# Input units in 64-row halves beside the scores: an attention and bilinear feed-forward kernel on one Trainium2 core

## The chip, the cores and the metric

The kernel runs on one core of a Trainium2 chip. The time is the device time in microseconds (us) of one execution, and lower is better. Before the change, the median of six executions is 417.81 us (415.93 to 419.45).

Engines are named as the profile names them: PE is TensorE (matmuls, transposes), PEld its loading of weights, DVE is VectorE, ACT is ScalarE, POOL is GpSimd, SP is SyncE. POOL and SP here mostly issue DMA transfers. PE writes only to PSUM, which has eight banks, each of 128 partitions by 512 fp32 values.

## The reference

```
B, H, S, D = 8, 8, 576, 64                      # q, k, v: [B, H, S, D]
scores = (q @ k^T) / sqrt(D) + bias[bucket(|i-j|)]   # one bias table a head
attn   = exp(scores - max) / sum
x      = (attn @ v) laid out as [B*S, H*D] = [4608, 512]
out    = ((x @ w_a) * (x @ w_b)) @ w_out         # d_model 512, d_ff 1536
```

## The kernel before, in words

**Pairs and slots.** Two heads of a batch entry make a pair; there are 32 pairs (`NP`), four to a batch entry. The loop over `s` from 4 to 32 is what this text calls slots: slot `s` computes the scores of pair `s` and the weighted values (`av`) of pair `s - 1`. The sequence of 576 is cut into four blocks of 128 and a tail of 64.

**Scores of a pair.** `qk1(p, t)` (line 334) multiplies key block `t` with all 512 queries, for the two heads at once: head 0 lies on partitions 0 to 63 and head 1 on 64 to 127, so there are two matmuls of 64 rows, one for each half of PE's rows, into two banks (line 342). `qk(p, t0)` does two blocks. `ex` (line 353) takes the exponential on ACT into a bf16 tile `at` of a pool of 8. `mul` (line 361) multiplies a band of it by exp(bias) on DVE. The `sc` pool has two buffers of two banks each.

**Tail.** `qk_tail` (lines 364 to 375) takes the main keys against the tail queries (line 367: four matmuls of 128 rows and 128 columns, both heads in one matmul, the operand padded with zeros), the tail keys against the main queries (line 370: one of 512 columns), and tail against tail (line 373: two of 64 columns into a bank `qktt`). `ex_tail` takes the exponentials of `qktt` and of the rest, `mul_tail` applies the bias. For pairs below 12 `qktt` lies in the bank TR, from 12 (`R3`) on in AV.

**Values and norm.** `av(p, jq)` (lines 403 and 412) multiplies the exponentials with v and a column of ones, for query blocks 0 to 2 into one bank and 3 to 4 into another. `norm` divides by the sums on DVE (a reciprocal on line 448, a product on line 449) into `XG`. `t_x` transposes `XG` into the feed-forward input `xn`: on PE with copies (`c_x`) for the first pairs, with DMA transposes on SP's queue for pairs 8 to 30 (`XD`). `t_q`, `c_q`, `t_k` and `c_k` make the transposed q and k of the next pair in PE for the first three batch entries (up to slot 10); later ones come from DMA transposes (`turn`).

**Feed-forward units.** There are nine chunks of 512 tokens (eight batch entries without their tails, and one of all tails). A chunk has 24 input units (`ff_a` and `ff_b` for each of 12 blocks of d_ff) and 12 output units (`ff_o`, four token blocks in three parts). Each unit is four matmuls of 128 rows and 512 columns. An a unit ends with ACT's copy `ha` out of PSUM (line 518), a b unit with the product `g = pb * ha` on DVE (line 523), and the third part of an output block with ACT's copy `ob` (line 546) and a store on SP's queue. There is one set of 12 tiles `g`, and the units run in one fixed order, chunk by chunk.

**Order.** Nothing schedules: the order in which instructions are written out is the order on each engine. The list `steps` of each slot mixes the attention steps with places `U`, and a quota of units (9 a slot from slot 9 on) is spread over these places. In slots 5 to 31 the scores come in two runs: `qk(s, 0)`, some units and av blocks, `qk(s, 2)`, more units and steps, then the tail. What is left of the units after the last slot runs by itself at the end.

**Banks.** Eight PSUM banks: four for `sc`, one AV, one TR, two FF. Units use the two FF banks in turn, and from slot 12 on (`ring3`) also TR for every third.

Of the kernel before, what the change touches and what calls it, by code (L numbers as in the profile page):

```python
# [13 lines left out]
def kernel(  # L14
# [11 lines left out]
    nc = tc.nc  # L26
# [22 lines left out]
    obp = ctx.enter_context(tc.tile_pool(name="obp", bufs=4))  # L49
    atp = ctx.enter_context(tc.tile_pool(name="atp", bufs=8))  # L50
    ps_sc = ctx.enter_context(tc.tile_pool(name="ps_sc", bufs=2, space=bass.MemoryType.PSUM))
# [57 lines left out]
    NW = 3  # L109
    R3 = 12  # L110
    WC = DF // NW
# [3 lines left out]
    xn_sb = [wpool.tile([128, 3 * SM + ST * B], BF16, name=f"xn{mc}") for mc in range(NMC)]  # L115
    g_sb = [wpool.tile([128, DM], BF16, name=f"g{df}") for df in range(NDF)]

# [149 lines left out]
    def kTt_(p):  # L267
        b, hp = divmod(p, 4)
        return KT[p % 2][:, SM:SM + 128] if early(b) else KTt[b % 2][:, hp, :]
# [9 lines left out]
    def bank(where, dt, name):  # L279
        return where[0].tile([128, 512 if dt is FP32 else 1024], dt, tag=where[1], name=name)  # L280
# [83 lines left out]
    def qk_tail(p):  # L364
        ps = ps_sc.tile([128, 2, 512], FP32, tag="sc", name=f"qkt{p}")
        for t in range(NM):
            nc.tensor.matmul(  # L367
                out=ps[:, 0, :].rearrange("p (h t c) -> p h t c", h=2, t=NM)[:, :, t, :],
                lhsT=kT_(p, t), rhs=qTt_(p), start=True, stop=True)
        nc.tensor.matmul(out=ps[:, 1, :], lhsT=kTt_(p), rhs=qT_(p), start=True, stop=True)  # L370
        pt = bank(TR if p < R3 else AV, FP32, f"qktt{p}")
        for hh in range(2):
            nc.tensor.matmul(out=pt[:, 0:ST], lhsT=kTt_(p), rhs=qTt_(p)[:, ST * hh:ST * hh + ST],  # L373
                             start=(hh == 0), stop=(hh == 1))
        st[p]["ps"] = (ps, pt)

    def ex_tail(p):
        ps, pt = st[p]["ps"]
        at = att_sb[p % 2]
        nc.scalar.activation(out=at[:, 1024:1024 + ST], in_=pt[:, 0:ST], func=ACTF.Exp, scale=scale)  # L380
        nc.scalar.activation(out=at[:, 0:1024].rearrange("p (a x) -> p a x", a=2),  # L381
                             in_=ps[:, :, :], func=ACTF.Exp, scale=scale)

# [109 lines left out]
    ring3 = False  # L493
    turn3 = 0

    def ff_bank(name):
        nonlocal turn3
        where = FF
        if ring3:
            turn3 += 1  # L500
            where = TR if turn3 % 3 == 0 else FF
        return where[0].tile([128, 512], FP32, tag=where[1], name=name)

    MC = (0, 1, 2, 3)

    def ff_mm(c, df, w, key, m0, m1):
        if m0 == 0:
            ff[key] = ff_bank(f"{key}{c}_{df}")
        for i in range(m0, m1):
            mc = MC[i]  # L510
            nc.tensor.matmul(out=ff[key][:, :], lhsT=w[df // FW][:, mc, 128 * (df % FW):128 * (df % FW) + 128],  # L511
                             rhs=xn_sb[mc][:, xin(c)],
                             start=(i == 0), stop=(i == NMC - 1))

    def ff_a(c, df, m0=0):
        ff_mm(c, df, wa_sb, "pa", m0, NMC)
        ha = wrk.tile([128, 512], FP32, tag="ha", name=f"ha{c}_{df}")
        nc.scalar.activation(out=ha[:, :], in_=ff["pa"][:, :], func=ACTF.Copy)  # L518
        ff["ha"] = ha

    def ff_b(c, df, m0=0):
        ff_mm(c, df, wb_sb, "pb", m0, NMC)
        nc.vector.tensor_tensor(out=g_sb[df][:, :], in0=ff["pb"][:, :], in1=ff["ha"][:, :], op=MULT)  # L523

    def ff_last(c, tt):
        ob = obp.tile([128, DM], FP32, tag="ob", name=f"ob{c}_{tt}")
        for x, cols in enumerate((slice(0, 256), slice(256, 512))):
            po = ff_bank(f"po{c}_{tt}_{x}")
            for df in range(NDF):
                nc.tensor.matmul(out=po[:, cols], lhsT=g_sb[df][:, 128 * tt:128 * tt + 128],  # L530
                                 rhs=wo_sb[:, df, cols], start=(df == 0), stop=(df == NDF - 1))
            copy(None if x else nc.scalar, ob[:, cols], po[:, cols])
            for hh, eng in enumerate((nc.sync, nc.scalar)):
                r0 = S * (2 * tt + hh) + SM
                eng.dma_start(out=out[r0:r0 + ST, cols], in_=ob[64 * hh:64 * hh + 64, cols])

    def ff_o(c, tt, part):
        if part == 0:
            ff["po"] = ff_bank(f"po{c}_{tt}")
        po = ff["po"]  # L540
        for df in range(4 * part, 4 * part + 4):
            nc.tensor.matmul(out=po[:, :], lhsT=g_sb[df][:, 128 * tt:128 * tt + 128],  # L542
                             rhs=wo_sb[:, df, :], start=(df == 0), stop=(df == NDF - 1))
        if part == 2:
            ob = obp.tile([128, DM], FP32, tag="ob", name=f"ob{c}_{tt}")
            nc.scalar.activation(out=ob[:, :], in_=po[:, :], func=ACTF.Copy)  # L546
            if c < B:
                r0 = S * c + 128 * tt
                nc.sync.dma_start(out=out[r0:r0 + 128, :], in_=ob[:, :])
            else:  # L550
                for hh in range(2):
                    r0 = S * (2 * tt + hh) + SM
                    nc.sync.dma_start(out=out[r0:r0 + ST, :], in_=ob[64 * hh:64 * hh + 64, :])

    units = []
    def last(part):
        if part == 0:
            ff_last(NCH - 1, 3)

    for c in range(NCH):  # L560
        for df in range(NDF):
            m0 = 3 if c == 0 and df == 0 else 0
            units.append(lambda c=c, df=df, m0=m0: ff_a(c, df, m0))
            units.append(lambda c=c, df=df, m0=m0: ff_b(c, df, m0))
        for tt in range(4):
            for part in range(3):
                if c == NCH - 1 and tt == 3:
                    units.append(lambda part=part: last(part))
                else:
                    units.append(lambda c=c, tt=tt, part=part: ff_o(c, tt, part))  # L570
    nxt = 0

    def put_units(n):
        nonlocal nxt
        for _ in range(n):
            units[nxt]()
            nxt += 1

    ACT = nc.scalar
# [134 lines left out]
    norm(3, 3)  # L714
    ff_mm(0, 0, wa_sb, "pa", 0, 3)
    t_x(3, AV, range(3))
    t_x(3, AV, range(3, 5))
    ff_mm(0, 0, wb_sb, "pb", 0, 3)
    c_x(3)
# [16 lines left out]

    quotas = {4: 12, 5: 7, 6: 6, 7: 4, 8: 4}
    for s in range(4, NP + 1):
        new = s < NP
        U = "unit"  # L740
        A = lambda *jq: (lambda: [av(s - 1, j, AV if j < 3 or s >= R3 else TR) for j in jq])
        N = lambda j: (lambda: norm(s - 1, j))
        steps = []
        if s == R3:
            ring3 = True
        if s == 4:
# [4 lines left out]
                      lambda: mul_tail(4), U, lambda: t_q(5, TR), lambda: c_q(5), U,  # L751
                      lambda: t_k(5, AV), lambda: c_k(5), U, U]
        elif new:
            e = early((s + 1) // 4)
            steps += [lambda: qk(s, 0), lambda: ex(s, 0), U, lambda: ex(s, 1), A(0, 1, 2), N(0), U,
                      lambda: mul(s, 0)]
            av34 = [A(3, 4), N(3)]
            if s - 1 in XD:
                av34 += [lambda: t_x(s - 1), lambda: turns(s)]
            if s < R3:  # L760
                steps += av34
            steps += [U, lambda: mul(s, 1)]
            if s >= R3:
                steps += av34
            steps += [lambda: qk(s, 2), lambda: ex(s, 2), U]
            if e:
                steps += [lambda: t_q(s + 1, TR), lambda: c_q(s + 1)]
            steps += [lambda: ex(s, 3), U, lambda: mul(s, 2)]
            if e:
                steps += [lambda: t_k(s + 1, AV), lambda: c_k(s + 1)]  # L770
            steps += [U, lambda: mul(s, 3), lambda: qk_tail(s), lambda: ex_tail(s), U]
            if s - 1 not in XD:
                steps += [lambda: t_x(s - 1, TR), lambda: c_x(s - 1), lambda: turns(s)]
            steps += [U, lambda: mul_tail(s), U]
        else:
            steps += [A(0, 1, 2), N(0), U, A(3, 4), N(3), U, lambda: t_x(s - 1, AV),
                      lambda: c_x(s - 1), U, U, U, U, U, U, U]
        quota = quotas.get(s, 9)
        seen, put = 0, 0
        nu = sum(1 for x in steps if x is U)  # L780
# [47 lines left out]
```

## Time and profile before

| | |
|---|---|
| median of six executions | 417.81 us |
| the profiled execution | 415.93 us, of which the span from the first to the last instruction is 414.2 us |
| mean granted TensorE clock | 0.999 of full speed |
| busy PE / PEld / DVE / ACT / POOL | 403.2 / 207.9 / 197.2 / 245.1 / 119.4 us |
| start of slot 9 (its first score matmul) | 79.8 us |
| start of slots 10, 11, 12, 13 | 91.5, 103.3, 114.5, 125.6 us |
| start of slot 31 | 324.7 us |

The groups that matter, by line (mean length of one instruction, not the distance between two):

| line, engine | what | count | mean ns |
|---|---|---|---|
| 342 PE | scores, 64 rows by 512 columns | 256 | 382 |
| 511, 542 PE | units, 128 rows by 512 columns | 1231 | 380 |
| 367 PE | tail scores, 128 rows by 128 columns | 128 | 220 |
| 412 PE | values, 128 rows by 65 columns | 1248 | 193 |
| 353 ACT | exp of scores, 128 by 1024 | 128 | 1023 |
| 518 ACT | copy `ha`, 128 by 512 | 108 | 598 |
| 380 ACT | exp of `qktt`, 128 by 64 | 32 | 224 |
| 523 DVE | product `g`, 128 by 512 | 108 | 692 |
| 361 DVE | bias product, 128 by 512 / 128 by 768 | 64 / 64 | 418 / 551 |

The length of a matmul in the profile includes its way through the array, and the next one starts before it ends. How fast PE gets on is therefore read from the distances of starts. A few per cent of matmul records are missing from the trace, which looks like a gap of one matmul.

### The profile page before, as it was taken

What the parts mean: (1) busy time and instruction counts of PE and PEld (TensorE: products, weight loads), DVE (VectorE), ACT (ScalarE), POOL (GpSimd) and SP (SyncE); (2) the same over time, 40 slices, a digit from 0 to 9 for tenths busy, and PEclk for the clock granted to TensorE, in tenths of its full rate; (3) what the DMA queues carried; (4) which work ended last, traced back from release to release, by engine and by line L of the source; (5) the groups of instructions that cost most, each with busy time, mean ns of one, the idle gap of its engine ahead of it and who ended that gap; (6) DMA issues with size and microseconds to landing.
All of it is one profiled execution on the core that took longest, in us unless ns stands there. A gap on an engine that the chain in (4) does not pass through costs nothing.

```text
span 414.2 us, 8425 instructions
## 1 busy us (share of the span) xinstructions
PE 403.2 (97%) x3350; PEld 207.9 (50%) x3407; DVE 197.2 (48%) x485; ACT 245.1 (59%) x345; POOL 119.4 (29%) x161
## 2 busy tenths in 40 slices
PE   8899999999999999999999999999999999999996
PEld 3573555645555545555455445555555554444443
DVE  3785676556533555255524563455435540430430
ACT  4987576766766666566667665776567632322321
POOL 9989729905447001820082003000000000000000
PEclk9999999999999999999999999999999999999999
DMA  9999999999959911999099909811120002002004
GB/s 160 195 174 164 161 174 153 171 161 95 132 63 183 166 35 36 140 168 119 16 130 199 110 16 86 179 35 39 41 90 15 3 17 101 2 0 102 2 0 101
DMA packets 164935, 40.75 MB, mean 98 GB/s; under 512 B 155320, under 2 KB 160224, under 8 KB 164896
## 3 DMA queue, kind: packets, MB, share of 16 engines
q0 software_dynamic: 110448, 18.75, 64.9%
q1 hardware_dynamic: 53168, 21.03, 27.4%
q10 hardware_dynamic: 1280, 0.43, 0.5%
q8 instruction: 26, 0.43, 0.4%
q14 instruction: 13, 0.11, 0.1%
HBM read 38.77 MB, written 9.45 MB: 116 GB/s over the span
## 4 chain that ended last, share of the span: by engine, by line
PE 94%; DMA 2%; issue 1%; ACT 1%; DVE 1%; SPq 0%; ACTq 0%
PE pa L511 23%; PE pb L511 22%; PE po L542 22%; PE av L412 9%; PE qk L342 8%; PE av L403 2%; PE qkt L367 2%; PE qkt L370 1%; DMA kt<-in_k_dram 1%; DMA k<-in_k_dram 1%; ACT at L353 1%; PE trx L475 1%; PE po L530 1%; PE qktt L373 1%; PE trq L291 0%
## 5 line engine op out<-in xcount | busy, mean ns | idle before, releaser
L353 ACT ACTIVATE at<-qk 128x1024 bf16<-128x1024 f32 x128 | 126.2, 1023 | 24.0 <-PE qk L342 24.0
L523 DVE TENSOR_TENSOR g<-pb,ha 128x512 bf16<-128x512 f32 x108 | 74.7, 692 | 116.9 <-PE pb L511 101.5
L511 PE MATMUL pa<-xn,wa 128*128 128x512 bf16 x417 | 110.2, 380 | 1.1 <-issue 0.3
L511 PE MATMUL pb<-xn,wb 128*128 128x512 bf16 x411 | 109.2, 380 | 1.1 <-issue 0.2
L518 ACT ACTIVATE ha<-pa 128x512 f32<-128x512 f32 x108 | 64.6, 598 | 66.4 <-PE pa L511 65.8
L542 PE MATMUL po<-wo,g 128*128 128x512 bf16 x403 | 96.3, 380 | 1.1 <-issue 0.3
L511 PEld LDWEIGHTS <-wa 128*128 128x128 bf16 x432 | 39.1, 98 | 49.6 <-issue 9.2
L511 PEld LDWEIGHTS <-wb 128*128 128x128 bf16 x432 | 39.2, 98 | 47.8 <-issue 7.1
L361 DVE TENSOR_TENSOR at<-at,W 128x512 bf16<-128x512 bf16 (+1 forms) x128 | 59.1, 484 | 7.1 <-ACT at L353 5.5
L542 PEld LDWEIGHTS <-g 128*128 128x128 bf16 x420 | 37.8, 98 | 46.4 <-issue 7.4
L546 ACT ACTIVATE ob<-po 128x512 f32<-128x512 f32 x35 | 20.9, 597 | 60.7 <-PE po L542 58.8
L123 POOL DMA_DIRECT2D vm<-in_v_dram x32 | 28.2, 925 | 98.4 <-PE av L412 61.3
L412 PE MATMUL av<-vm,at 128*128 128x65 bf16 x992 | 43.3, 193 | 0.0
L412 PEld LDWEIGHTS <-at 128*128 128x128 bf16 x992 | 39.4, 97 | 6.2
L448 DVE RECIPROCAL rc<-av 128x6 f32<-128x6 f32 x64 | 12.0, 188 | 54.5 <-PE av L412 52.9
L403 PE MATMUL av<-vt,att 128*128 128x130 bf16 x156 | 34.7, 223 | 0.0
L381 ACT ACTIVATE att<-qkt 128x1024 bf16<-128x1024 f32 x32 | 32.6, 1020 | 0.0
L449 DVE TENSOR_TENSOR XG<-av,rc 128x384 bf16<-128x384 f32 x64 | 31.4, 491 | 2.4 <-DVE rc L448 0.2
L123 POOL DMA_DIRECT2D qn<-in_q_dram x28 | 24.4, 923 | 23.7 <-PE trq L291 16.2
L123 POOL DMA_DIRECT2D kn<-in_k_dram x28 | 24.5, 919 | 4.8 <-DMA vt<-in_v_dram 2.4
L342 PE MATMUL qk<-QTb,KTb 64*128 64x512 bf16 x160 | 24.2, 382 | 0.0
L403 PEld LDWEIGHTS <-att 128*128 128x128 bf16 x156 | 15.3, 98 | 7.4 <-issue 0.7
(121 smaller groups left out, 242.0 us busy)
## 6 DMA issues: line engine op xcount, KB each, us to landing
out_dram<-ob SPq DMA_DIRECT2D x32, 256.0 KB, 4.1
vm<-in_v_dram POOLq DMA_DIRECT2D x28, 128.0 KB, 5.8
qn<-in_q_dram POOLq DMA_DIRECT2D x24, 128.0 KB, 9.1
kn<-in_k_dram POOLq DMA_DIRECT2D x24, 128.0 KB, 9.4
wa<-in_moe_w_a_dram POOLq DMA_DIRECT2D x3, 512.0 KB, 7.0
wb<-in_moe_w_b_dram POOLq DMA_DIRECT2D x3, 512.0 KB, 9.7
wo<-in_moe_w_out_dram POOLq DMA_DIRECT2D x1, 1536.0 KB, 13.3
W<-bias_tab POOLq DMA_DIRECT2D x4, 192.0 KB, 5.1
```

The source lines that it names most:

```text
L123: nc.gpsimd.dma_start(out=(vm[b % 2][:, h0:h1, t, 0:Dh] if dst is None else dst[b % 2][:, :].rearrange("p (t h d) -> p t h d", h=H, t=NM)[ ...
L342: nc.tensor.matmul(out=ps[:, hh, :], lhsT=kT_(p, t)[r, :], rhs=qT[r, :, :], start=True, stop=True)
L353: nc.scalar.activation(out=at[:, :, :], in_=ps[:, :, :], func=ACTF.Exp, scale=scale)
L361: nc.vector.tensor_tensor(out=at[:, :, lo:hi], in0=at[:, :, lo:hi], in1=w[:, :, y:(None if z < 0 else z):-1], op=MULT)
L381: nc.scalar.activation(out=at[:, 0:1024].rearrange("p (a x) -> p a x", a=2), in_=ps[:, :, :], func=ACTF.Exp, scale=scale)
L403: nc.tensor.matmul(out=pav[:, slot, :, :], lhsT=x, rhs=vt[b // 2 % 2][:, 4 * i + hp, :, 0:Dh + 1], start=fresh, stop=True, skip_group_chec ...
L412: nc.tensor.matmul(out=pav[:, slot, hh, :], lhsT=x, rhs=vm[i][:, 2 * hp + hh, t, 0:Dh + 1], start=False, stop=True, skip_group_check=True)
L449: nc.vector.tensor_tensor(out=xg[:, j0:j0 + n, :, :], in0=pav[:, 0:n, :, 0:Dh], in1=rc.unsqueeze(3).to_broadcast([128, n, 2, Dh]), op=MULT)
L511: nc.tensor.matmul(out=ff[key][:, :], lhsT=w[df // FW][:, mc, 128 * (df % FW):128 * (df % FW) + 128], rhs=xn_sb[mc][:, xin(c)], start=(i = ...
L518: nc.scalar.activation(out=ha[:, :], in_=ff["pa"][:, :], func=ACTF.Copy)
L523: nc.vector.tensor_tensor(out=g_sb[df][:, :], in0=ff["pb"][:, :], in1=ff["ha"][:, :], op=MULT)
L542: nc.tensor.matmul(out=po[:, :], lhsT=g_sb[df][:, 128 * tt:128 * tt + 128], rhs=wo_sb[:, df, :], start=(df == 0), stop=(df == NDF - 1))
```

## The change

**What it does.** From slot 9 (`R4`) on, a slot begins with `run`: the four score blocks of the pair and the matmuls of four input units, all with 64 rows. Each unit matmul of 128 rows is split into its lower and its upper 64 rows, which add up in the same bank. Two units go together, one in an FF bank, the other in AV (first two) or TR (last two): `begin` writes the lower halves of the one beside the upper halves of the other, `end` the two remaining sets. Between them the copy `hop` on DVE reads one value of a bank of `begin`, and the matmuls of `end` wait for it. Then come the tail scores, the main keys by 64-row halves, two matmuls a key block of 64 columns, in the same run; line 370's matmul becomes two of 256 columns; and `qktt` lies in AV. The bank layout of the tail scores changes, and `ex_tail` writes them to the same places.

After it come the rest of the units as whole matmuls, the values of the pair before, and for slots 9 and 10 the transposes of the next pair. `plan` gives for each slot how many input and output units it has: 6 and 3, but (4, 3), (6, 0), (5, 0), (5, 0), (4, 3) in slots 9 to 13 and (6, 0) in slot 17. That is 189 units in slots 9 to 31, against 207 before; the other 18 run at the end. Input units are now ahead of output units by up to a chunk and a half, so there are two sets of `g`, the second one in the tiles `q32` and `k32`, which are used only in the first slots. `atp` has 10 buffers, not 8. The use of TR by every third unit (`ring3`) starts in slot 32. In slot 8 the transposes of pair 7 (`t_x`, `c_x`) come earlier in the slot.

```diff
+    def wide(p):
+        return p >= R4
...
     def qk_tail(p):
         ps = ps_sc.tile([128, 2, 512], FP32, tag="sc", name=f"qkt{p}")
-        for t in range(NM):
+        if wide(p):
+            for t in range(NM):
+                for hh in range(2):
+                    r = slice(64 * hh, 64 * hh + 64)
+                    nc.tensor.matmul(out=ps[:, hh, ST * t:ST * t + ST], lhsT=kT_(p, t)[r, :],
+                                     rhs=qTt_(p)[r, ST * hh:ST * hh + ST], start=True, stop=True)
+            for x in range(2):
+                nc.tensor.matmul(out=ps[:, x, 256:512], lhsT=kTt_(p), rhs=qT_(p)[:, 2 * x:2 * x + 2, :],
+                                 start=True, stop=True)
+        for t in range(NM if not wide(p) else 0):
...
-        pt = bank(TR if p < R3 else AV, FP32, f"qktt{p}")
+        pt = bank(AV if wide(p) else TR, FP32, f"qktt{p}")
...
+    def put_in(us, where):
+        nonlocal here
+        for u in us:
+            here = where
+            for x in u_mms(u):
+                mm(x)
+            here = None
+            u_end(u)
+
+    def begin(x, y):
+        nonlocal here
+        got = []
+        for u, where in (x, y):
+            here = where
+            got.append(u_mms(u))
+        here = None
+        for p, q_ in zip(*got):
+            mm(p, lo)
+            mm(q_, hi)
+        nc.vector.tensor_copy(out=hop[:, :], in_=got[1][0][0][0:1, 0:1])
+        return got
+
+    def end(x, y, got):
+        for p, q_ in zip(*got):
+            mm(q_, lo, False, True, True)
+            mm(p, hi, False, True, True)
+        for u in sorted((x[0], y[0]), key=lambda u: (u[2], u[0])):
+            u_end(u)
+
+    def run(s, us):
+        u, v_ = [sorted(x, reverse=True) for x in (us[0:2], us[2:4])]
+        u, v_ = list(zip(u, (FF, AV))), list(zip(v_, (FF, TR)))
+        qk1(s, 0)
+        ex(s, 0)
+        got0 = begin(*u)
+        qk1(s, 1)
+        ex(s, 1)
+        got1 = begin(*v_)
+        qk1(s, 2)
+        ex(s, 2)
+        end(*u, got0)
+        qk1(s, 3)
+        ex(s, 3)
+        end(*v_, got1)
...
+    plan = {9: (4, 3), 10: (6, 0), 11: (5, 0), 12: (5, 0), 13: (4, 3), 17: (6, 0)}
...
+        A = lambda *jq: (lambda: [av(s - 1, j, AV if j < 3 or s == NP else TR) for j in jq])
...
+        elif new and s >= R4:
+            e = early((s + 1) // 4)
+            n_in, n_out = plan.get(s, (6, 3))
+            four, rest, o = take(ins, 4), take(ins, n_in - 4), take(outs, n_out)
+            X = lambda us: [lambda: put_in(us, FF)]
+            TQ = [lambda: t_q(s + 1, TR), lambda: c_q(s + 1)] if e else []
+            TK = [lambda: t_k(s + 1, TR), lambda: c_k(s + 1)] if e else []
+            first = o[0:1] or rest[0:1]
+            rest = rest if o else rest[1:]
+            steps += [lambda: run(s, four), lambda: qk_tail(s), lambda: put_in(first, FF), lambda: ex_tail(s),
+                      lambda: mul(s, 0)] + TQ + X(o[1:2]) + [lambda: mul(s, 1)]
+            steps += TK + X(o[2:]) if o else []
+            steps += [A(0, 1, 2), N(0)]
+            steps += [] if o else TK
+            steps += X(rest[0:1]) + [lambda: mul(s, 2), A(3, 4), N(3), lambda: t_x(s - 1), lambda: turns(s)]
+            steps += X(rest[1:2]) + [lambda: mul(s, 3), lambda: mul_tail(s)]
```

`u_mms` lists a unit's matmuls, `u_end` writes its copy, product or store, `lo` and `hi` are partitions 0 to 63 and 64 to 127, `put_in` is a unit of whole matmuls, `X` one such place, `A` an av block, `N` a norm.

## The prediction

> **What bounds the kernel now.** I read the page first: the engines' busy time and the chain that ended last.
>
> ```profile
> span 414.2 us, 8425 instructions
> ...
> PE 403.2 (97%) x3350; PEld 207.9 (50%) x3407; DVE 197.2 (48%) x485; ACT 245.1 (59%) x345; POOL 119.4 (29%) x161
> ...
> PEclk9999999999999999999999999999999999999999
> ...
> PE 94%; DMA 2%; issue 1%; ACT 1%; DVE 1%; SPq 0%; ACTq 0%
> ```
>
> TensorE (PE) is 94% of the chain at full granted clock, and the other engines are little over half busy. So time comes off only where TensorE issues less or loses less between its matmuls, and every new TensorE wait is paid in full. Busy time cannot show the losses, since a record lasts 0.38 us where matmuls follow every 0.2155 us. So next I read starts of matmuls, in the timeline of one slot (a slot is one pair of heads, here slot 20): of PE, then of ACT and DVE in the same slot. Columns: start and length in us, engine, line, operation, count.
>
> ```profile
> 213.74 0.38 PE L542 MATMUL po<-wo,g 128*128 128x512 bf16 x1
> 214.05 0.39 PE L342 MATMUL qk<-QTb,KTb 64*128 64x512 bf16 x2
> ...
> 218.45 0.40 PE L412 MATMUL av<-vm,att 128*128 128x65 bf16 x8
> 218.79 0.60 PE L342 MATMUL qk<-QTb,KTb 64*128 64x512 bf16 x4
> 219.33 1.04 PE L511 MATMUL pa<-xn,wa 128*128 128x512 bf16 x4
> 220.20 1.02 PE L511 MATMUL pb<-xn,wb 128*128 128x512 bf16 x4
> 221.06 1.03 PE L511 MATMUL pa<-xn,wa 128*128 128x512 bf16 x4
> 221.93 0.39 PE L367 MATMUL qkt<-QTt,KTb 128*128 128x128 bf16 x4
> 222.15 0.38 PE L370 MATMUL qkt<-QTb,KTt 128*128 128x512 bf16 x1
> ```
>
> ```profile
> 220.40 0.60 ACT L518 ACTIVATE ha<-pa 128x512 f32<-128x512 f32 x1 [0.16 <-PE pa L511]
> 220.90 1.02 ACT L353 ACTIVATE at<-qk 128x1024 bf16<-128x1024 f32 x1
> ...
> 222.63 0.22 ACT L380 ACTIVATE att<-qktt 128x64 bf16<-128x64 f32 x1
> ```
>
> ```profile
> 221.34 0.69 DVE L523 TENSOR_TENSOR g<-pb,ha 128x512 bf16<-128x512 f32 x1 [1.80 <-PE pb L511]
> ```
>
> Four matmuls of a unit take 0.86 us (220.20 to 221.06), so one takes 0.2155. Around the 64-row scores there is a loss. From the last 128-row matmul at 213.74 to the first 64-row one at 214.05 are 0.31 us: 0.095 too many. The four 64-row matmuls of 218.79 run as two pairs, each two matmuls in the time of one (0.431 for both), yet the next unit starts 0.54 later: 0.11 too many. The unit after it starts 0.87 later, not 0.86: 0.01. One 64-row run costs 0.21 us over its work, and each slot has two. Between them TensorE does not wait: slots 13 to 31 are 11.06 us apart ((324.7 - 125.6)/18, starts of line 342). Only slots 9, 10 and 11 each show one gap of 0.15 us:
>
> ```profile
> 89.77 0.81 PE L511 MATMUL pa<-xn,wa 128*128 128x512 bf16 x3
> 90.56 1.02 PE L511 MATMUL pb<-xn,wb 128*128 128x512 bf16 x4
> ```
>
> (last start 89.77 + 0.81 - 0.38 = 90.20, next 0.36 later, 0.15 over the step).
>
> **The change, part by part, for its 23 slots (9 to 31).**
>
> *One 64-row run in place of two.* Saves 23 x 0.21 = 4.8 us. The tail halves continue this run, so the way back to 128 rows is still paid once.
>
> *Tail scores in halves.* The four matmuls of line 367 take 0.22 us (221.93 to 222.15). After it, four pairs of 64 columns. No row shows such a pair. If the two run together as in line 342, a pair takes 0.029 (the step of the 65-column matmuls of line 412: eight in 0.24 us) plus the 3 to 4 ns between the starts of a 342 pair, 0.033; if they do not, 0.058. I take the first, the nearest row in form: saving 0.22 - 0.13 = 0.09 a slot, 2.0 us; bounds 2.4 and -0.3. The Trainium skill (TensorEngine Tiling (Array Packing), Instruction Overhead) speaks against it: about 60 cycles of overhead for each matmul, so tiling should not be bought from a dimension that is already small. By the 65-column row the step at 65 columns is 0.029 us; an estimate by the page, eight matmuls of 64 columns that do not gain from pairing, would make this term nearly zero. One matmul of 512 columns as two of 256 adds nothing (the 24 of line 530 step by 0.109).
>
> *Sixteen unit matmuls as 16 pairs of halves.* Same columns streamed, if pairs follow every 0.2155 us. From the first matmul of the last pair in a run to the next 128-row one are 0.312 us, against 0.311 the other way, so a pair costs some 1 ns more than one matmul: 16 x 23 x 0.001 = 0.4 us lost. Bounds: zero, and the distance of the two pairs of a run, 0.227 us; but the first two 128-row matmuls after a run also are 0.226 apart, so I read that as a cost of starting. If it held for each pair: 4.2 us. That pairs accumulate into two banks at once is shown nowhere here.
>
> *The added copy `hop` and its waits.* The second halves wait for a VectorE copy that waits for the first halves. Four pairs and two scores lie between (6 x 0.2155 = 1.3 us); VectorE's last work of a slot (line 361, 387, 390: 0.33 + 0.16 + 0.14 between starts, behind a g of 0.61) ends some 1.8 us into the next, the wait is at 2.4. Zero; without this cover some 0.2 us each. Behind a late hop would queue the g products, and behind them the banks.
>
> *The first 128-row unit of a slot waits for a bank.* It takes the FF bank of the first b unit. Counting from the first score: pair n starts at 0.227 + 0.2155(n - 1). Third score (pair 10) 2.17; plus 0.42 to its exp (start to ACT as at 218.79 and 219.22) 2.59; the a unit's copy follows 0.90 later (the least distance of two ACT starts after an exp in the trace) at 3.49, ends 4.09; g starts 0.03 later, takes 0.69; TensorE resumes 0.06 after: 4.87. TensorE gets there at 0.227 + 19 x 0.2155 + 0.13 + 0.095 + 0.23 + 0.06 = 4.84. Wait 0.03 x 23 = 0.8 us; zero if the tail halves are slow, 1.3 if they are at their best.
>
> *The tail bank moves to AV, and a copy gets ahead of it.* In slots 10, 11 and 17, which have no output units, the first 128-row unit is an a unit, and its copy stands ahead of the tail's exp in ScalarE's in-order queue. The next av matmuls want the AV bank that this exp frees. From the unit's last start: 0.38 to its end, 0.04, 0.49 for the copy's step, 0.22 for exp (222.63), 0.05 to TensorE: 1.18, of which 0.2155 is its own step. TensorE stands 0.97 us in slots 11 and 17, and 0.75 in slot 10, where four transposes (0.22) come between: 2.7 us. Nothing hides it; the units that would have are moved to the end.
>
> *AV and TR now also hold a units.* In a full slot norm's products are done over 0.5 us before. Slots 9 to 13 have only 5 to 7 units: VectorE lags. Worked through in the same way, slot 13's first a unit waits 0.7 us for norm of slot 12 (three g of 0.61 and two multiplies of 0.33 and 0.46 stand ahead); slot 10 waits 0.3 for the K copy in TR; five others 0.13 or less: 1.6 us. In slot 9 the exps start late behind the tail of slot 8: 0.3. Together 1.9, bounds 0.5 and 3.
>
> *Hidden or neutral.* Eighteen units move from the slots to the end, where units also step by 0.86: zero. The second set of g removes a wait that TensorE does not have. POOL's v loads and the transposes on SP (3.5 us to landing) leave later in the slot, behind av, at most 6 us, with a slot or more to spare; the output stores on SP keep their count. The 0.15 gaps of slots 9 to 11 go: 0.45 us gained.
>
> **Sum.** 4.8 + 2.0 + 0.45 - 0.4 - 0.8 - 2.7 - 1.9 = 1.5 us. Span 414.2 to 412.7; the profiled execution took 415.93, so 414.4. That one was the fastest of six; on their median of 417.81: **416.3 us**.
>
> **Rivals.**
> *The waits of the short slots vanish* (ScalarE gets through earlier, or TensorE fills in): then 4.8 + 2.0 + 0.45 - 0.4 - 0.8 = 6.1, that is 411.7 us. For it: ScalarE is 59% busy. Against: its queue is in order, and the copy needs a unit that TensorE has only just finished. Chance 0.18.
> *Halves pace slower* (the other side): pairs in the run follow every 0.227 us as the measured two do, because the second load of weights or accumulation into two banks is not hidden. Price 4.2 in place of 0.4, and with the tail pairs unpaired 2.3 less a returned 0.8: the sum falls to -3.8, 421.6 us; without the tail part 420.1. It decides from 5 ns a pair, where the gain of 1.5 is gone. Against it: the weights of the second pair are loaded 11 ns after the first pair starts. The skill (TensorE: Matmul & The Clock Gate, Measured speedup vs the span model) has some 4 ns per tile and 3.07 times for four row tiles, not 4. The trace has 1 ns a pair; by the page's 4 ns, an estimate, this term would be 1.5 us and the gain nearly zero. Chance 0.25.
> *The halves do not run side by side at all*: 16 x 23 x 0.2155 = 79 us, 495 us. Pairs of line 342 start 3 to 4 ns apart, against it. Chance 0.02.
>
> **How the numbers follow.** The forecast has 0.55. A difference of 0.5% (2.1 us) is about what a measurement of this kernel can tell from none. The forecast's own range by its bounds is a gain of 3.5 to a loss of 1, with three tenths of it above 2.1. Faster: 0.18 + 0.17 = 0.35. Within: most of the rest of the forecast, 0.35, and the milder part of the slow rival, 0.05: 0.40. Slower: 0.25. Range 412.8 to 420.0: up to near the first rival, down into the second.
>
> **What would show it.** One 64-row stretch a slot with 20 pairs 0.2155 us apart; full slots some 10.8 us long for nine units; gaps near 1 us ahead of line 423 in slots 11 and 17, ended by the tail's exp; one of 0.7 in slot 13 ended by VectorE. Pairs of 0.22 us or more, or full slots over 11 us, would make it wrong on the slow side; no gaps in slots 10 to 17 on the fast side.

## The result, and the profile after

The changed kernel takes 415.22 us (median of 21 executions, 414.09 to 416.26), the kernel before 417.40 (median of 47). The ratio is 0.9948, with a 95% interval of 0.9938 to 0.9959: 2.2 us less. The forecast was 1.5 us less than a median of 417.81, 416.3 us, in a range of 412.8 to 420.0.

These lines of the changed kernel's page stand for the ones shown of before. Of them the chain looks different; the busy shares hardly moved.

```profile
span 414.2 us, 9454 instructions
...
PE 399.7 (97%) x3831; PEld 219.3 (53%) x3890; DVE 201.2 (49%) x531; ACT 243.9 (59%) x345; POOL 119.3 (29%) x161
...
PE 79%; DMA 11%; POOL 6%; issue 2%; DVE 1%; ACT 1%; POOLq 0%; DVEq 0%
```

Its span is that of before, 414.2 us, though the medians differ by 2.2. The two profiled executions stand at different ends of their kernels' scatter: before's was the fastest of 47 (415.93), the changed kernel's (415.97) among its slower ones. The DMA and POOL shares of the chain point to a load that came late ahead of slot 9. By the starts of the slots, slot 9 begins 2.67 us later: 0.79 of it lie ahead of slot 4, 1.26 in slot 7, where the transposes of K wait for the load of kn, and 0.62 in slot 8; the experiments come back to the last two. So the stretches are compared by the start of the first score matmul of each slot.

| | before | after |
|---|---|---|
| start of slot 9 | 79.75 | 82.42 |
| slot 9 to the end | 334.41 | 331.77 |
| slot 8 | 7.58 | 8.20 |
| slots 9 to 13 (before 45 units, after 30, the other 15 at the end) | 56.87 | 45.22 |
| a full slot (mean of 19 to 25) | 11.062 | 10.794 |
| slot 17 (9 units, after 6) | 11.06 | 9.16 |

The timeline of the changed kernel's slot 20 shows the run (columns as above; the places where two halves go together are two lines with one start):

```profile
190.93 0.39 PE L347 MATMUL qk<-QTb,KTb 64*128 64x512 bf16 x2
191.16 0.38 PE L538 MATMUL pb<-xn,wb 64*128 64x512 bf16 x1
191.16 0.38 PE L538 MATMUL pa<-xn,wa 64*128 64x512 bf16 x1
191.38 0.38 PE L538 MATMUL pb<-xn,wb 64*128 64x512 bf16 x1
191.38 0.38 PE L538 MATMUL pa<-xn,wa 64*128 64x512 bf16 x1
...
195.26 0.28 PE L375 MATMUL qkt<-QTt,KTb 64*128 64x64 bf16 x8
195.47 0.39 PE L378 MATMUL qkt<-QTb,KTt 128*128 128x256 bf16 x2
195.70 0.22 PE L388 MATMUL qktt<-QTt,KTt 128*128 128x64 bf16 x2
195.81 1.02 PE L538 MATMUL po<-wo,g 128*128 128x512 bf16 x3
```

Pairs start 0.216 us apart: in the 16 slots from 15 on whose halves all start together (all but slot 18), the first distance of a run is 0.226 us, and the other 304 are 215 to 217 ns, 215.8 in the mean, as are the distances of whole matmuls before. So a pair of halves costs what one whole matmul costs. The four pairs of tail halves step by 0.028 to 0.029 us, the pace of single matmuls of 65 columns before. There is one way in and one way out of the 64 rows a slot. `po` starts 0.05 us later than it could.

In slot 13 the first halves do not start together:

```profile
118.10 0.38 PE L538 MATMUL pb<-xn,wb 64*128 64x512 bf16 x1
118.80 0.39 PE L538 MATMUL pa<-xn,wa 64*128 64x512 bf16 x1 [0.32 <-DVE XG L469]
```

The half of the a unit was due beside the b half at 118.10. It came 0.70 us later, when the norm product on DVE had read its bank, AV. Over the step of 0.2155, the distance between the two starts is 0.48 us too long.

### The profile page after: what moved, and what is told of

Same layout as the page of the kernel before. It is cut to its first block, busy times and chain, and to the rows that moved or that the text cites. A ratio compares the mean times of both kernels' runs of the same rounds, so it can differ in the third digit from the quotient of the medians.

```text
span 414.2 us, 9454 instructions
## 1 busy us (share of the span) xinstructions
PE 399.7 (97%) x3831; PEld 219.3 (53%) x3890; DVE 201.2 (49%) x531; ACT 243.9 (59%) x345; POOL 119.3 (29%) x161
## 4 chain that ended last, share of the span: by engine, by line
PE 79%; DMA 11%; POOL 6%; issue 2%; DVE 1%; ACT 1%; POOLq 0%; DVEq 0%
PE po L538 21%; PE pa L538 20%; PE pb L538 20%; PE av L432 7%; PE qk L347 5%; DMA wb<-in_moe_w_b_dram 5%; DMA qn<-in_q_dram 3%; DMA vm<-in_v_dram 2%; PE av L423 2%; PE qkt L378 2%; DMA kn<-in_k_dram 1%; PE qkt L375 1%; PE po L555 1%; POOL vt L150 1%; POOL ktl L150 1%
## 5 line engine op out<-in xcount | busy, mean ns | idle before, releaser
L538 PE MATMUL pb<-xn,wb 64*128 64x512 bf16 (+1 forms) x592 | 156.7, 378 | 1.3
L538 PE MATMUL pa<-xn,wa 128*128 128x512 bf16 (+1 forms) x609 | 157.2, 378 | 0.7 <-DVE XG L469 0.3
L538 PEld LDWEIGHTS <-wa 64*128 64x128 bf16 (+1 forms) x616 | 56.6, 96 | 44.3 <-DVE XG L469 2.3
L538 PEld LDWEIGHTS <-wb 64*128 64x128 bf16 (+1 forms) x616 | 56.8, 96 | 41.1 <-issue 1.5
L548 DVE TENSOR_TENSOR g<-pb,ha 128x512 bf16<-128x512 f32 x60 | 41.5, 692 | 65.2 <-PE pb L538 38.0
L538 PE MATMUL po<-wo,g 128*128 128x512 bf16 x216 | 51.8, 379 | 0.6
L548 DVE TENSOR_TENSOR q<-pb,ha 128x512 bf16<-128x512 f32 x32 | 22.1, 692 | 41.8 <-ACT ha L544 21.0
L538 PEld LDWEIGHTS <-g 128*128 128x128 bf16 x228 | 21.4, 98 | 22.9 <-issue 0.7
L347 PE MATMUL qk<-QTb,KTb 64*128 64x512 bf16 x160 | 32.1, 379 | 0.0
L538 PE MATMUL po<-wo,q 128*128 128x512 bf16 x116 | 29.6, 379 | 0.6
```

The source lines that it names most:

```text
L347: nc.tensor.matmul(out=ps[:, hh, :], lhsT=kT_(p, t)[r, :], rhs=qT[r, :, :], start=True, stop=True)
L538: return nc.tensor.matmul(out=o[:, :], lhsT=w[r, :], rhs=m[r, :], start=first if start is None else start, stop=final if stop is None else ...
L548: nc.vector.tensor_tensor(out=g_sb[c % 2][df][:, :], in0=ff.pop(("pb", df))[:, :], in1=ff.pop(("ha", df))[:, :], op=MULT)
```

## The experiments

Each kernel is the changed one with the edit shown. Times are medians; a profile's stretch from slot 9 to the end stands beside them, since it leaves out the loads at the start.

**The waits for the AV bank.** In slot 11 of the changed kernel, PE and then ACT:

```profile
107.04 1.02 PE L538 MATMUL pa<-xn,wa 128*128 128x512 bf16 x3
108.86 0.22 PE L423 MATMUL av<-vt,att 128*128 128x130 bf16 x1 [0.80 <-ACT att L395]
```

```profile
108.10 0.60 ACT L544 ACTIVATE ha<-pa 128x512 f32<-128x512 f32 x1 [0.43 <-PE pa L538]
108.59 0.22 ACT L395 ACTIVATE att<-qktt 128x64 bf16<-128x64 f32 x1
```

The last start of the unit is 107.04 + 1.02 - 0.38 = 107.68, the next matmul comes 1.18 later, 0.96 over the step. (The 0.80 in brackets counts from the modelled end of the unit.) ACT sat idle for 0.43 us while the exp that TensorE needs, whose scores had been ready since about 107.2, stood behind the unit's copy. The edit writes that exp first:

```diff
-steps += [lambda: run(s, four), lambda: qk_tail(s), lambda: put_in(first, FF), lambda: ex_tail(s),
+steps += [lambda: run(s, four), lambda: qk_tail(s), lambda: ex_tail(s), lambda: put_in(first, FF),
```

> The tail's exps are written ahead of the first whole unit, so that in slots 10, 11 and 17 ScalarE takes the exp of qktt before the unit's copy; nothing else differs from the changed kernel. Theory (the copy ahead of the exp holds the AV bank): the gaps of 0.74, 0.96 and 0.96 us ahead of the av matmuls in slots 10, 11 and 17 go, some 0.2 us come back as waits of the next slot for norm, so 2.4 us less than the changed kernel, 412.8 us, ratio to before 0.989. Rival (the gaps only move, because these slots are short of units and VectorE or the score buffers hold TensorE next): less than 0.7 us gained, 414.5 or more.

Measured: 414.26 us, ratio 0.9928 (0.9903 to 0.9952). Slots 10, 11 and 17 became 0.53, 0.96 and 0.95 us shorter, 2.44 together, as the theory says (slot 10 kept a wait of 0.43 us, for the K copy). But slot 12 went from 7.41 to 8.91 us, and slot 9 to the end fell only from 331.77 to 330.82. The time went here, in slot 12 of this experiment:

```profile
112.85 0.49 PE L375 MATMUL qkt<-QTt,KTb 64*128 64x64 bf16 x8
114.67 0.39 PE L378 MATMUL qkt<-QTb,KTt 128*128 128x256 bf16 x2 [1.33 <-DMA KTt<-ktl]
```

KTt, the transposed tail of the keys of batch entry 3, comes by a DMA transpose on SP's queue. The kernel before issues it at 100.40, and it lands 7.4 us later, 14.8 ahead of its first reader at 122.59. Here it was issued at 105.91 and landed 8.7 us later. In the changed kernel it was issued at 107.01 and landed 8.0 later, about when its first reader started, at 115.1: no wait to be seen, and no slack either. Neither theory had this wait: 1.4 us by the length of the slot, since 0.095 of the distance between these rows is the usual way from 64 to 128 rows.

**That transpose issued a slot earlier**, with the exps first:

```diff
-        if 2 < b < B and s % 4 < 3:
+        if 2 < b < B and s % 4 < 3 and s != 10:
             turn(b, "qkt"[s % 4])
+        if s == 9:
+            turn(3, "t")
```

> The exps ahead of the first unit, as in the first of these experiments, and the DMA transposes of the tails of batch entry 3 (QTt, KTt) written in slot 9 and not slot 10. Theory (in that experiment the 2.4 us of slots 10, 11 and 17 were gained, and 1.5 us given back in slot 12, where the tail scores now come before KTt has landed, because the change issues this transpose behind the av blocks of slot 10): the wait of 1.49 us in slot 12 goes, slot 12 lasts 7.5 us and not 8.9, 1.4 us less than that experiment, 412.9 us, ratio 0.989. Rival (the transposes are slow because of the loads around them, wherever they are issued, or push back K's): slot 12 stays above 8.5 us, 414 us or more.

Measured: 412.67 us, ratio 0.9898 (0.9881 to 0.9915); slot 12 lasts 7.51 us, slot 9 to the end 329.42. The transposes landed in 6.1 us from 98.5. The wait was one of lateness.

**Slot 8.** The change had moved the transposes of pair 7 (`X1`: `t_x`, `c_x` and `turns`). In the changed kernel:

```profile
77.35 0.81 PE L538 MATMUL po<-wo,g 128*128 128x512 bf16 x3
78.47 0.45 PE L495 MATMUL trx<-cst_sb,XG 128*128 128x128 bf16 x5 [0.30 <-DVE XG L469]
78.85 0.60 PE L347 MATMUL qk<-QT,KT 64*128 64x512 bf16 x4
79.54 0.40 PE L296 MATMUL trq<-cst_sb,qn 128*128 128x128 bf16 x4
```

The transposes start 0.47 us late, waiting for norm. The next ones start 0.24 us late by their distance; 0.09 of it is the way from 64 to 128 rows, which the kernel before pays there too, and 0.15 the wait for the copy out of the same bank. Together that is 0.62 us. The edit puts the old place back:

```diff
-            steps += X1 if s == R4 - 1 else []
...
-            steps += X1 if s < R4 - 1 else []
+            steps += X1
```

> Slot 8 only: the transposes of pair 7 and their copies go back to the end of the slot, as in the kernel before. Theory (the earlier place costs two waits, 0.47 us for norm and 0.24 us for the copy, and the fourth group of the first units reads this input late enough anyway): 0.7 us less than the changed kernel, 414.5 us. Rival (the first units of slot 9 then wait for the copies, which is what the earlier place avoids): same time or up to 0.5 us more, 415.2 to 415.7, with a new gap after the first score of slot 9.

Measured: 414.74 us, ratio 0.9935 (0.9913 to 0.9956), 0.5 us under the changed kernel by the medians, which these intervals alone do not separate. The profile does: slot 8 lasts 7.58 us, as before, and not 8.20, and the 0.62 between them is the sum of the two waits; slot 9 has no new gap and lasts 9.75. In the other experiments that keep the early place slot 8 lasts 8.20 each time. This version also came early enough to slot 12 to wait 0.08 us for KTt (a distance of 0.18 over the work, of which 0.095 is the usual way).

**The tail halves alone undone.** Lines 371 to 400 take their old branches, and AV stays the bank of `qktt`:

```diff
     def qk_tail(p):
-        if wide(p):
+        if False:
...
-        for t in range(NM if not wide(p) else 0):
+        for t in range(NM):
```

> The tail scores again as four matmuls of 128 rows and 128 columns and one of 512 (the exponentials again in the old layout), all else as in the changed kernel. Theory (halves run in pairs, 0.029 us a pair): the tail takes 0.222 in place of 0.116 us, 23 times, 2.4 us more, of which the bank wait after the tail gives back 0.053 us in some 20 slots, 1.1 us: 1.3 us more than the changed kernel, 416.5 us. Rival (the 64-column halves are bound by a cost per matmul and gain nothing): same time within 0.3 us.

Measured: 416.09 us, ratio 0.9966 (0.9954 to 0.9978), 0.9 us more than the changed kernel; slot 9 to the end 332.99, 1.22 us more. In its slot 21:

```profile
205.62 0.40 PE L381 MATMUL qkt<-QTt,KTb 128*128 128x128 bf16 x4
205.85 0.38 PE L385 MATMUL qkt<-QTb,KTt 128*128 128x512 bf16 x1
206.06 0.22 PE L388 MATMUL qktt<-QTt,KTt 128*128 128x64 bf16 x2
206.12 2.75 PE L538 MATMUL po<-wo,g 128*128 128x512 bf16 x11
```

`po` follows `qktt` by 0.06 us, with no wait; a full slot lasts 10.85 us. The halves save 0.11 us a slot, and the bank wait behind them takes half of it back.

**The unit halves undone.** Four whole units, one after each score block:

```diff
     def run(s, us):
-        u, v_ = [sorted(x, reverse=True) for x in (us[0:2], us[2:4])]
...
-        end(*v_, got1)
+        for t, (u, where) in enumerate(zip(us, (AV, FF, TR, FF) if us[0][0] == "a" else (FF, AV, FF, TR))):
+            qk1(s, t)
+            ex(s, t)
+            put_in([u], where)
```

> The four input units beside the scores as whole matmuls of 128 rows, one after each score block, at the same places and in the same banks, without the copy hop. The scores and the tail halves are then five 64-row runs a slot in place of one. Theory (each run costs 0.21 us over its work, and the halves are worth just the runs they save): 4 x 0.21 x 23 = 19.3 us more, less some 1.1 us of the bank wait after the tail, 18 us more than the changed kernel, 433 us. Rival (the gain over before comes from elsewhere, the second set of g or the halves' pace, and the way between 64 and 128 rows hides behind the loading of weights): under 8 us more.

Measured: 433.35 us, ratio 1.0385 (1.0364 to 1.0406). A full slot lasts 11.60 us, 0.81 more than the changed kernel's. The timeline of its slot 21 shows why:

```profile
210.19 0.39 PE L347 MATMUL qk<-QTb,KTb 64*128 64x512 bf16 x2
210.51 1.04 PE L538 MATMUL pa<-xn,wa 128*128 128x512 bf16 x4
211.48 0.39 PE L347 MATMUL qk<-QTb,KTb 64*128 64x512 bf16 x2
```

One score pair and four matmuls of 0.2155 us are 1.08 us of work, and they come every 1.29: 0.21 lost each time. The gain over before comes from the number of runs and, for a smaller part, from the tail halves; unit halves as such gain nothing.

**The kernel before once more.**

> The kernel before once more, for a second profile. The profiled execution of before was the fastest of 47 (415.93 us against a median of 417.4), and its slot 7 starts 7.58 us before slot 8; the four other profiles, all of later versions that have the same code up to slot 7, show 8.2 to 9.0 us there, with a wait of the K transposes for the load of kn. If that wait depends on the execution and not on the change, slot 7 lasts 8.2 us or more here too and the span is 1 us or more above 414.2; from slot 9 to the end 334.4 us, as in the first profile. If the change causes it, slot 7 lasts 7.6 us.

Measured: a span of 415.9 us, in an execution of 418.43. Slot 9 to the end is 334.43 us, as in the first profile (334.41). Slot 7 lasts 7.88, so the expectation of 8.2 missed; but slot 5 lasts 11.15 where the first profile has 10.17, with the same kind of wait:

```profile
53.10 0.23 PE L311 MATMUL trk<-cst_sb,kn 128*128 128x128 bf16 x1 [0.19 <-DMA kn<-in_k_dram]
```

The waits of slots 5 and 7 for the load of kn change from execution to execution, with and without the change (slot 7 lasts 7.6 to 9.0 us in the profiles), so they are not counted as its effect. Of the eight profiles with the change five show 8.2 us or more in slot 7, three 7.6 to 7.8; the two of before show 7.6 and 7.9. Whether the change makes the waits likelier these few profiles do not settle.

**All three edits together.**

> The exps ahead of the first unit, the tail transposes of batch entry 3 in slot 9, and the transposes of pair 7 back at the end of slot 8. Theory (three separate waits): the gains add, 2.4 and 0.6 us less than the changed kernel, 412.2 us, ratio 0.9875; gaps left are 0.1 and 0.4 in slot 10 and 0.5 in slot 13. Rival (as the pair comes on earlier, the next DMA transpose or the K load of slot 7 sets the pace of slots 8 to 12): 413 us or more.

Measured: 412.01 us, ratio 0.9876 (0.9859 to 0.9892), the best version. Slot 9 to the end is 329.42 us, as with two edits, and slot 8 lasts 7.58 us. The waits of TensorE from slot 9 to slot 31 that its profile still names:

```profile
PE pa L538 <- DVE XG L469: 0.3, 1, 0.3
PE av L423 <- DVE KT L262: 0.3, 1, 0.3
```

The columns after the colon are us in total, times, and the longest. By the distances of starts they are 0.48 us in slot 13 and 0.43 in slot 10.

**Norm ahead of the bias products**, in the slots without output units, to remove these two:

```diff
-                      lambda: mul(s, 0)] + TQ + X(o[1:2]) + [lambda: mul(s, 1)]
+                      ] + ([lambda: mul(s, 0)] if o else []) + TQ + X(o[1:2]) + ([lambda: mul(s, 1)] if o else [])
...
-            steps += [] if o else TK
+            steps += [] if o else TK + [lambda: mul(s, 0), lambda: mul(s, 1)]
```

> All three edits of the best version so far, and in the slots without output units (10, 11, 12, 17) the first two bias products stand behind norm in VectorE's queue and not ahead of it. Theory (the waits of 0.48 us in slot 13 for norm of slot 12, and of 0.43 in slot 10 for the K copy behind norm, come from 0.8 us of bias products ahead of norm): both go or fall below 0.1, 0.8 us less, 411.2 us, ratio 0.9855; slots 9 to the end 328.6 us where the version without it has 329.4. Rival (the three products g ahead of norm in slot 12 are what holds it): the gap of slot 13 stays above 0.3 and the time the same within 0.3 us.

Measured: 413.68 us, ratio 0.9912 (0.9885 to 0.9940); slot 9 to the end 331.00 us, 1.58 more than without it. Neither theory held: the wait of slot 13 grew, and the time with it.

```profile
108.84 0.38 PE L538 MATMUL pb<-xn,wb 64*128 64x512 bf16 x1
109.70 0.39 PE L538 MATMUL pa<-xn,wa 64*128 64x512 bf16 x1 [0.49 <-DVE XG L469]
```

This is the second a unit of slot 12's run, in TR. The second half of norm, which frees TR, now stood behind three bias products in a row. In the version without this edit DVE does two of them ahead of norm, while TensorE makes the first av blocks; here it sat idle there for 0.61 us, and did them between the two halves of norm. The wait for the K copy in slot 10 went from 0.43 to 0.31 us. The distances between starts show new waits of 0.21 us in slot 11, 0.65 in slots 12 and 13 each (0.48 in slot 13 without this edit) and 0.38 in slot 18, and a half that runs without its partner adds a step. By their lengths slots 10 to 13 take 35.10 us together where they took 34.07, and slot 18 takes 11.39 where it took 10.83: 1.59, the whole loss.

## Why the prediction was right, step by step

The sign was right, and the mechanism: 1.5 us forecast, 2.2 measured, with the signs that were named (one 64-row stretch a slot, full slots of 10.8 us, gaps near 1 us in slots 11 and 17 and of 0.7 in slot 13). That the total is so near is in part luck: two parts came out some 0.6 us better each, and one that the sum left out cost 0.6. The slot that the prediction shows is slot 21, not 20; all full slots are alike, and nothing hangs on it. The steps:

- *One run less, 4.8 us.* Right. Taking the units out of the run cost 0.81 us a slot for four more runs, and four times 0.21 less the bank wait of 0.05 is 0.79.
- *Tail halves, 2.0 us.* The nearer bound held: 0.028 to 0.029 us a pair, 0.11 us a slot, 2.4 us. The rule of the Trainium skill on small dimensions (TensorEngine Tiling (Array Packing), Instruction Overhead), as I had read it, for eight matmuls that gain nothing, does not fit: two of 64 columns in two row halves took the time of one.
- *Halves of units, -0.4 us.* Less than 1 ns a pair (215.8 against 215.8), nothing to be seen. 0.226 us is the distance behind the first pair of a run only, as read. The 4 ns per tile of the Trainium skill (TensorE: Matmul & The Clock Gate, Measured speedup vs the span model) are here the distance of starts within a pair (3 to 4 ns), and are not added to the distance of pairs.
- *The wait for the first b unit's bank, -0.8 us.* 0.05 and not 0.03 us a slot, 1.1 us. With the three terms above, a full slot was to last 10.8 us and lasts 10.794.
- *The copy `hop`, zero.* Right: in slot 20 it ends at 192.49, and the matmul that waits for it starts at 193.32.
- *The exp behind a copy in slots 10, 11 and 17, -2.7 us.* Right, 0.74, 0.96 and 0.96 us. Writing the exp first removed 2.44 us from these slots.
- *The gaps of 0.15 us in slots 9 to 11, 0.45 us gained.* Right, the distances of starts show none of them any more.
- *Banks AV and TR in short slots, -1.9 us.* The two large waits came as forecast (0.70 and 0.31 us against 0.7 and 0.3), the late exps of slot 9 did not: about 1.3 us in all. Slot 13 lasts 9.77 us, where a full slot less two units is 10.794 - 2 x 0.862 = 9.07: 0.70 lost, 0.48 of it as a distance between starts and a step of 0.2155 because a half of the b unit had gone ahead without its partner. Slot 10 loses 0.31, all the others about 0.3.
- *Slot 8.* Missing. The sum has no term for the move of pair 7's transposes, so it counts the move as free; it costs 0.62 us. It lies ahead of the 23 slots that I summed.
- *Transposes on SP that leave later, zero.* Zero in this kernel, but "a slot or more to spare" was wrong. KTt left 6.6 us later (2.7 of it because slot 9 began later in this profile), but its reader also came 7.5 us earlier (115.13, not 122.59), which the prediction did not count; and the 3.5 us to landing were the median of the `xn` transposes, where KTt took 7.4 in the kernel before. So the 14.8 us to spare were gone, and KTt landed as it was needed. The next gain ran into it and lost 1.4 us there.

Over the stretch from slot 9 to the end the change gains 2.64 us where 1.5 was forecast. Of the 1.14 between them 0.6 are the full slots (23 x 0.268 = 6.2 us, against 4.8 + 2.0 - 0.4 - 0.8 = 5.6) and some 0.6 the banks and the exps of slot 9 (1.9 less 1.3); 6.2 + 0.45 - 2.7 - 1.3 is 2.65. It gives back 0.62 in slot 8, which leaves 2.0, against 2.2 by the medians.

The rival of vanishing waits was wrong, since the waits are there; but most of them came from the order of writing and were no price of the change, which is why 412.0 us could be had; 0.7 in slot 13 and 0.4 in slot 10 are left. The slow rival fell with its premise: pairs follow every 0.216 us.

## What to carry to other kernels

When one engine is busy throughout, take the distances of its starts in one period, list every distance over the work's own, and ask which kind of neighbours makes it; here two 64-row runs a slot cost 0.42 of 11.06 us, 4% of the time, and dividing other work into halves so that it fits into one run cost nothing that could be seen. Then look at the periods that are not full: the order that hides all but 0.05 us behind nine units showed gaps of 0.3 to 1 us in slots with five to seven. And when a step is moved later, compare its landing with its reader, which may have moved too, by a number, because a transfer that still just arrives will stop the next improvement.

## What the runs showed that was not expected

- A DMA transpose that lands in 2.7 us (median of five such transposes of KTt in the profile with the exps first) took 7.0 to 8.7 us when it was issued in slot 11, while POOL issued the q, k and tail loads of the next batch entry, and 6.1 to 6.8 us when the same edit issued it a slot earlier (6.2 and 7.4 in the two profiles of the kernel before, also in slot 10). That the loads slow it down no run shows by itself.
- Two profiles of the kernel before differ by 1.75 us ahead of slot 9, and by 0.02 us over the 334.4 us after it. Its median, 1.5 us above the first profile's execution, may come from there; the other executions have no profile.
- Where one half waits for its bank, the partner written ahead of it goes alone, and the pairing is lost for a step: the wait costs 0.2155 us more than the gap between starts shows (slot 13, 0.70 for 0.48). Halves that are only out of step, as in slot 14, where they start 0.130 and 0.086 us apart in turn, lose no more than the first delay, 0.12 us there: each half still follows its like every 0.216 us.
